# Two sums of attention weights per pair of heads: formed in the weights' own tiles, partly by DMA, with the mask of two pairs on another engine

## The chip, the cores and the metric

The kernel runs on one core of a Trainium2 chip. The metric is the device time of one execution in microseconds (us). A profiled execution also leaves a trace: the start and the length of every instruction on TensorE (PE, and PEld for its weight loads), VectorE (DVE), ScalarE (ACT), GpSimd (POOL) and SyncE (SP), and of every DMA packet.

## The reference

Hashed attention is followed by a mixing layer. Only the first part is touched by the change.

```python
# q, k, v: (4, 8, 768, 64), proj: (64, 6)
q_bucket = sum((q @ proj > 0) * 2**arange(6));  k_bucket likewise
mask   = q_bucket[..., :, None] == k_bucket[..., None, :]
scores = where(mask, q @ k.T / sqrt(64), -1e9)
attn   = exp(scores - max) / (sum(exp(scores - max)) + 1e-9)
x      = (attn @ v), heads side by side: (4, 768, 512)
# then: X = real(fft2(x)); u = x + X; un = layernorm(u)
# out = u + relu(un @ w_ch1) @ w_ch2      w_ch1: (512, 2048), w_ch2: (2048, 512), both float64
```

## The kernel before

**Pairs and chunks.** Two heads make a pair: 4 batches of 4 pairs, numbered n = 0 to 15. `attention(b)` loops over the four pairs of a batch and, in each, over six chunks c of 128 keys. One such step does this:

- `weigh(n, c)`: PE forms the transposed scores, 128 keys by 2 x 384 queries for each head (L815); ACT takes the exponential into a weights tile `pk` of 128 x 1536 numbers (L819, two instructions). The mask comes in one of two ways. For the pairs in `LITE` (0 to 4) two more matmuls per half put a very large term under the scores of matching buckets (L808). For the others DVE multiplies the weights by a comparison of bucket numbers, two instructions per chunk (L825).
- `values`: PE multiplies the previous chunk's weights by v, into two accumulating banks (L836).
- DVE adds the chunk's weights to a running sum `acc` (L898): for batch 0 in two halves of 128 x 768, later in one instruction of 128 x 1536. Five chunks are added per pair, the first being the start.
- `prepare(n + 1)`: transposes, copies and bucket bits of the next pair's q and k, spread over the steps. A pair in `LITE` needs four matmuls and six DVE instructions for its bits (L735 to L742); another needs one bank of bits, two bucket images (L764, copied at L768) and one small table `kb`.
- One slice of the float64 weights is turned into float32 by `narrow`: DVE at L603, L607 and L612, ACT at L611, L615 and L616. w1 has 16 slices, done during `attention(0)` in four of five steps; w2 has 16, done later, during `attention(1)`.

After the last chunk `scale` adds up a pair: a copy `vs` on DVE (L845), two ACT copies that wait for it (L848), four matmuls of `acc` with ones (L853), and a quotient on DVE, two times six instructions from L859 to L869.

**Tiles.** There are two weights tiles (`NPK = 2`), used in turn, and two `acc` tiles in the work pool (tag `t6`, shared with the temporaries `ef` of `fold`).

**Order.** For `attention(0)` the order on PE, DVE, ACT and POOL is the order in which the program is written. Later the order is set by a planner with priorities, where `mix(b - 1)`, the mixing layer of the batch before, runs between the steps of `attention(b)`. Each engine works through its own list in order. `fold(b, 0)` begins the mixing inside the last pair of a batch.

**Queues.** SP issues the loads of q, k and v, the constants, the first seven slices of w1 and the stores of `ad` and `bd`. POOL issues the other 9 slices of w1 and all 16 of w2 (`fetch`, L657, 512 KB each), and the output.

Of the kernel before, what the change touches and what calls it, by code (L numbers as in the profile page):

```python
# [479 lines left out]
def _main(  # L480
# [27 lines left out]
    def wt(shape, dtype, tag, name, bufs=2):  # L508
        return work.tile(shape, dtype, tag=tag, name=name, bufs=bufs)
# [44 lines left out]
    make_identity(nc, ident)  # L554


    LITE = (0, 1, 2, 3, 4)
    pjw = const.tile([P, P], F32, tag="pjw", name="pjw")
    nc.gpsimd.memset(pjw, 0.0)
    for h in range(2):  # L560
# [13 lines left out]
    norms = const.tile([P, 2, NPAIR * B], F32, tag="norms", name="norms")  # L574


    NPK = 2
    pks = []
    for i in range(NPK):
        pk = const.tile([P, 2, 2, HALF + 1], F32, tag=f"pk{i}", name=f"pk{i}")  # L580
# [52 lines left out]
    def weights(wsb, wdr):  # L633

        wide = wdr.dtype == I64
        slices = [
            (wsb[:, c, f : f + WC], wdr[c * P : (c + 1) * P, f : f + WC])
            for f in range(0, wdr.shape[1], WC)
            for c in range(wdr.shape[0] // P)
        ]  # L640
        raws, masks = [], []
        if wide:
            zt = wt([P, 3, 2 * WC], F32, "z", f"zraw{wdr.shape[0]}", 1)
            raws += [zt[:, i] for i in range(3)]
            if wsb is w1:
                ft = wt([P, 12, WC], F32, "F", "fraw", 1)
                raws += [
                    ft[:, i : i + 2].rearrange("p i w -> p (i w)") for i in range(0, 8, 2)
                ]
                masks = [ft[:, i] for i in range(8, 12)]  # L650

        def fetch(i, queue):
            if i < len(slices):
                dst, src = slices[i]
                if wide:
                    raw = raws[i % len(raws)].bitcast(I32)
                    queue.dma_start(raw.bitcast(I64), src)  # L657
                else:
                    queue.dma_start(dst, src)

        depth = len(raws) or 4
        for i in range(depth):
            fetch(i, nc.sync if wsb is w1 else nc.gpsimd)
            if wsb is w1 and i == 1:
                load(1)
        yield
        for i, (dst, src) in enumerate(slices):
            if wide:
                mask = masks[i % 4] if masks else wt([P, WC], F32, "u", f"mask{i}", 2)
                narrow(  # L670
                    dst, raws[i % len(raws)].bitcast(I32), mask.bitcast(I32),
                    i if wsb is w1 else len(slices) + i,
                )
            fetch(i + depth, nc.gpsimd)
            yield
            if wsb is w1 and i % NDC == NDC - 1:


                f = i // NDC * WC
                if f < DFF // 2:  # L680
                    centre(f, average(f))
# [13 lines left out]
    def prepare(n):  # L695

        lite = n in LITE
        act = lite and n > 0  # L700
        ts = {}
        for io, nm in enumerate("qk"):
            tn = nat.pop((nm, n))
# [55 lines left out]
        for h in range(2):  # L759
            ps = ps_sc.tile([P, 2, 512], F32, tag="sc", name=f"qb{n}_{h}")  # L760
            for g in range(2):
                rows = slice(32 * g, 32 * g + 32)
                with behind() if g + h else nullcontext():
                    last[0] = nc.tensor.matmul(  # L764
                        ps[:, g, 0:HALF], pw[rows, h, :], bt[rows, :],
                        start=True, stop=True,
                    )
            evac(qb[:, h, :].rearrange("p (g s) -> p g s", g=2), ps[:, :, 0:HALF])  # L768
        ps = ps_sc.tile([P, 2, 512], F32, tag="sc", name=f"kb{n}")
        for c in range(NT):  # L770
            g, i = divmod(c, NT // 2)
# [9 lines left out]
        )  # L781
        preps[n] = ts["q"], ts["k"], qb, kb

    npk = [0]

    AHEAD = 500

    last = [None]
# [4 lines left out]
        with tc.issue_after(last[0].ins), tc.high_priority(offset=AHEAD):  # L793
            yield

    def weigh(n, c):

        qt, kt, qb, kb = preps[n]
        ks = slice(c * P, (c + 1) * P)
        heads = [slice(h * D, (h + 1) * D) for h in range(2)]  # L800
        pk = pks[npk[0] % NPK]
        npk[0] += 1
        for g in range(2):
            qs = slice(g * HALF, (g + 1) * HALF)
            ps = ps_sc.tile([P, 2, 512], F32, tag="sc", name=f"sc{n}_{g}_{c}")
            if kb is None:
                for h, rows in enumerate(heads):
                    nc.tensor.matmul(  # L808
                        ps[:, h, 0:HALF], qb[rows, 1, ks], qb[rows, 0, qs],
                        start=True, stop=False,  # L810
                    )

            for h, rows in enumerate(heads):
                with behind() if g + h and n >= NPAIR else nullcontext():
                    last[0] = nc.tensor.matmul(  # L815
                        ps[:, h, 0:HALF], kt[rows, ks], qt[rows, qs],
                        start=kb is not None, stop=True,
                    )
            nc.scalar.activation(  # L819
                pk[:, g, :, 0:HALF], ps[:, :, 0:HALF], AF.Exp, scale=SCALE  # L820
            )
        if kb is not None:
            for h in range(2):
                w = pk[:, :, h, 0:HALF]
                nc.vector.scalar_tensor_tensor(  # L825
                    w, qb[:, h].rearrange("p (g s) -> p g s", g=2), kb[:, h, c : c + 1], w,
                    op0=ALU.is_equal, op1=ALU.mult,
                )
        return pk

    def values(n, c, pk, oos):

# [5 lines left out]
                    pk[:, g, h, 0:w], start=(c == 0), stop=(c == NT - 1),  # L838
                )

    def scale(n, oos, acc):

        x = xs[n // NPAIR][:, n % NPAIR]
        vs = wt([P, 1], F32, "vs", f"vs{n}")
        nc.vector.tensor_copy(vs, oos[0][:, HALF : HALF + 1])  # L845
        halves = [x[:, g * HALF : (g + 1) * HALF] for g in range(2)]
        for g, xg in enumerate(halves):
            nc.scalar.activation(xg, oos[g][:, 0:HALF], AF.Identity, bias=vs)  # L848
        for g, xg in enumerate(halves):

            ps = pt([P, HALF], f"sum{n}_{g}")
            for h in range(2):
                nc.tensor.matmul(  # L853
                    ps[h * D : (h + 1) * D, :], ones, acc[:, g, h],
                    start=True, stop=True,
                )

            rt = wt([P, HALF], F32, "rt", f"rt{n}_{g}", 1)
            nc.vector.transpose(rt, ps)  # L859
            rc = wt([P, HALF // 32], F32, "rc", f"rc{n}_{g}")  # L860
            nc.vector.tensor_scalar(rc, rt[:, 0:HALF:32], S * EPS, None, op0=ALU.add)
            nc.vector.reciprocal(rc, rc)
            rb = wt([P, HALF], F32, "rb", f"rb{n}_{g}", 1)
            nc.vector.tensor_copy(
                rt.rearrange("p (j i) -> p j i", i=32),
                rc[:, :, None].broadcast_to([P, HALF // 32, 32]),
            )
            nc.vector.transpose(rb, rt)
            nc.vector.tensor_tensor(xg, xg, rb, op=ALU.mult)  # L869

    def attention(b):
# [1 line left out]
        pending = []  # L873

        def finish():
            n, c, pk, oos, acc = pending.pop(0)
            with behind() if n >= NPAIR and t is not None else nullcontext():
                values(n, c, pk, oos)
            if c == NT - 1:
                scale(n, oos, acc)  # L880

        for t in range(NPAIR):
            n = NPAIR * b + t
# [2 lines left out]
                load(n + 1)  # L886
            ahead = prepare(n + 1) if n + 1 < NPAIR * B else iter(())
            oos = [ps_o.tile([P, 512], F32, tag="o", name=f"oo{n}_{g}") for g in range(2)]
            acc = wt([P, 2, 2, HALF], F32, "t6", f"acc{n}", 2)
            first = None  # L890
            for c in range(NT):
                new = weigh(n, c)
                if c == 0:
                    first = new[:, :, :, 0:HALF]
                else:

                    for g in (0, 1) if b == 0 else (slice(0, 2),):
                        nc.vector.tensor_tensor(  # L898
                            acc[:, g], (first if c == 1 else acc)[:, g],
                            new[:, g, :, 0:HALF], op=ALU.add,  # L900
                        )
                while pending:
                    finish()
                pending.append((n, c, new, oos, acc))
                if c > 2:
                    next(half, None)
                if c > 0:
                    next(ahead, None)
                yield
        t = None  # L910
        while pending:
            finish()


    HW = HALF // 2
# [22 lines left out]
    def fold(b, cp):  # L938
# [4 lines left out]
        if cp == 0:  # L943
            zs[b] = wt([P, 2, 2, 2, HALF], F32, "z", f"z{b}", 1)
        for pc in range(2):
            ef = wt([P, 2, S], F32, "t6", f"ef{b}_{cp}_{pc}", 2)
            e = ef[:, 0]
            nc.vector.tensor_tensor(
                e, x[:, cp], x[:, cp + 2], op=ALU.subtract if pc else ALU.add
# [437 lines left out]
    next(other)  # L1387
    nc.sync.dma_start(ch, cn["ch"].ap())
    nc.sync.dma_start(sq, cn["sq"].ap())


    ET = mybir.EngineType
    with tc.manual_schedule(engines={ET.PE, ET.DVE, ET.Activation, ET.Pool}):
        for _ in prepare(0):
            pass
        roomy[0] = False
        for i, _ in enumerate(attention(0)):
            if i % 5 < 4:
                next(other, None)
        for _ in other:  # L1400
            pass
        pwf = wt([P, 2, P], F32, "t6", "pwf", 2)
        nc.sync.dma_start(pwf, cn["pw"].ap())
        nc.scalar.copy(pw, pwf)
        means = []
        for f in range(DFF // 2, DFF, WC):
            means.append((f, wt([P, WC], F32, "u", f"mean{f}", 2)))
# [92 lines left out]
```

## Time and profile before

| | us |
|---|---|
| median of three runs (1154.63 to 1157.35) | 1154.7 |
| profiled execution, its own time | 1154.21 |
| its span in the trace | 1152.4 |
| PE busy | 1100.6 (96%) |
| DVE busy | 779.9 (68%) |
| ACT busy | 451.8 (39%) |
| POOL busy | 74.5 (6%) |

The span is the time from the first to the last instruction of the program; 1.8 us of the profiled execution lie around it. An engine's busy time is the union of its instructions. A busy PE is one with matmuls in its pipeline and is not PE at its peak. A mean share says little here, since the kernel has stages with different limits; the pairs of batch 0 fill the stretch from 13.6 to 138.9 us, those of batch 1 the stretch to 412.9 us, if the first exponential of a pair is taken as its start.

### The profile page before, as it was taken

To read this page: it belongs to the slowest core of one execution; us is meant where nothing else is said; L and a number is where in the kernel's file an instruction comes from. 1 tells how busy PE (TensorE), PEld (TensorE's weight loads), DVE (VectorE), ACT (ScalarE), POOL (GpSimd) and SP (SyncE) were. 2 spreads that over 40 slices of the span, in tenths; PEclk is the share of its full clock that TensorE was granted. 3 is DMA by queue.
4 is the path that set the end of the run, shared out by engine and by line. 5 is a ranking of instruction groups with operands and counts; after the bars stand their busy time and mean duration, and the time that the engine had idled before them with its cause. 6 is when DMAs were issued, how large, how long until landed. Compare 5 with 4: busy or idle time off the path is not lost. (4 is left out here: it accounts for less than half of the span.)

```text
span 1152.4 us, 13749 instructions
## 1 busy us (share of the span) xinstructions
PE 1100.6 (96%) x4921; PEld 641.9 (56%) x4921; DVE 779.9 (68%) x1373; ACT 451.8 (39%) x858; POOL 74.5 (6%) x149
## 2 busy tenths in 40 slices
PE   7989889889999999999999999999999999999996
PEld 4444355444445445644674467654575468768675
DVE  4889959837938455883857877785775877644352
ACT  6778348623222212345224531345424431340420
POOL 1000001100100010020000002002000002010002
PEclk9999999999999999999999999999999999999998
DMA  9534135514611014113042315013104204131401
GB/s 272 151 80 121 40 93 168 167 44 146 224 48 47 17 32 152 28 51 106 15 151 68 86 52 177 15 42 96 47 31 139 64 28 164 48 96 56 154 24 39
DMA packets 131661, 103.11 MB, mean 89 GB/s; under 512 B 81280, under 2 KB 120320, under 8 KB 131584
## 3 DMA queue, kind: packets, MB, share of 16 engines
q1 hardware_dynamic: 123984, 82.35, 24.5%
q0 software_dynamic: 6032, 19.40, 5.1%
q8 instruction: 41, 0.67, 0.2%
q10 hardware_dynamic: 1568, 0.39, 0.2%
q14 instruction: 36, 0.29, 0.1%
HBM read 81.14 MB, written 20.97 MB: 89 GB/s over the span
## 5 line engine op out<-in xcount | busy, mean ns | idle before, releaser
L1214 PE MATMUL o<-w,h 128*128 128x256 f32 x864 | 194.0, 381 | 0.0
L819 ACT ACTIVATE pk<-sc 128x768 f32<-128x768 f32 x192 | 147.8, 808 | 101.2 <-PE sc L815 81.6
L1214 PEld LDWEIGHTS o<-w,h 128*128 128x128 f32 x864 | 162.3, 190 | 30.2 <-issue 3.4
L825 DVE SCALAR_TENSOR_TENSOR pk<-qb,kb,pk 128x768 f32<-128x768 bf16 x132 | 129.3, 1013 | 38.6 <-ACT pk L819 38.5
L815 PE MATMUL sc<-qt,kt 64*128 64x384 f32 x768 | 152.9, 501 | 0.9 <-ACT pk L819 0.9
L836 PE MATMUL oo<-pk,vn 128*64 128x385 f32 (+1 forms) x768 | 149.3, 498 | 1.8 <-DVE pk L825 1.8
L1314 PE MATMUL h_p<-x,w 128*128 128x384 f32 x384 | 140.2, 494 | 2.1 <-ACT qt L531 0.6
L898 DVE TENSOR_TENSOR acc<-acc,pk 128x1536 f32<-128x1536 f32 (+1 forms) x80 | 113.3, 1433 | 9.8 <-ACT pk L819 8.9
L1314 PE MATMUL h_p<-w 128*128 128x384 f32 x288 | 106.3, 492 | 2.9 <-ACT qt L531 1.8
L1314 PEld LDWEIGHTS h_p<-x,w 128*128 128x128 f32 x384 | 69.7, 190 | 56.5 <-ACT h L1346 3.4
L836 PEld LDWEIGHTS oo<-pk,vn 128*64 128x64 f32 x768 | 47.8, 136 | 90.5 <-issue 73.0
L1083 PE MATMUL h<-x,w 128*128 128x384 f32 x256 | 88.6, 499 | 4.1 <-DVE h L1089 3.1
L815 PEld LDWEIGHTS sc<-qt,kt 64*128 64x128 f32 x768 | 66.8, 186 | 44.7 <-issue 23.2
L1065 PE MATMUL o<-w,h 128*128 128x512 f32 x192 | 85.2, 596 | 0.6 <-DVE rt L859 0.6
L1314 PEld LDWEIGHTS h_p<-w 128*128 128x128 f32 x288 | 53.1, 190 | 43.4 <-ACT qt L531 2.4
L1083 PEld LDWEIGHTS h<-x,w 128*128 128x128 f32 x256 | 48.1, 193 | 40.6 <-issue 5.0
L1065 PEld LDWEIGHTS o<-w,h 128*128 128x128 f32 x192 | 35.5, 190 | 43.8 <-issue 41.7
L926 POOL DMA_DIRECT2D out_dram<-w x30 | 16.5, 552 | 468.7 <-issue 426.6
L1226 DVE SCALAR_TENSOR_TENSOR w<-o,rs,w 128x256 f32<-128x256 f32 x42 | 20.1, 481 | 32.2 <-PE o L1214 32.2
L1244 ACT COPY w<-o 128x256 f32<-128x256 f32 x18 | 6.7, 372 | 81.7 <-PE o L1214 81.7
L988 PE MATMUL cs<-ch,z 128*128 128x128 f32 (+3 forms) x192 | 31.8, 316 | 4.7 <-ACT kt L531 2.6
L1214 PE MATMUL o<-w 128*128 128x256 f32 x144 | 34.6, 383 | 1.2 <-DVE u L1226 0.9
(159 smaller groups left out, 1320.3 us busy)
## 6 DMA issues: line engine op xcount, KB each, us to landing
w<-ad SPq DMA_DIRECT2D x168, 128.0 KB, 2.0
w<-bd SPq DMA_DIRECT2D x42, 512.0 KB, 4.4
zraw<-in_moe_w_ch_dram POOLq DMA_DIRECT2D x21, 512.0 KB, 4.1
vn<-in_v_dram SPq DMA_DIRECT2D x32, 192.0 KB, 3.3
qn<-in_q_dram SPq DMA_DIRECT2D x31, 192.0 KB, 3.3
kn<-in_k_dram SPq DMA_DIRECT2D x31, 192.0 KB, 3.3
ad<-st SPq DMA_DIRECT2D x8, 512.0 KB, 3.7
bd<-st SPq DMA_DIRECT2D x8, 512.0 KB, 3.5
```

The costliest lines, as they stand in the source:

```text
L815: last[0] = nc.tensor.matmul(ps[:, h, 0:HALF], kt[rows, ks], qt[rows, qs], start=kb is not None, stop=True,)
L819: nc.scalar.activation(pk[:, g, :, 0:HALF], ps[:, :, 0:HALF], AF.Exp, scale=SCALE)
L825: nc.vector.scalar_tensor_tensor(w, qb[:, h].rearrange("p (g s) -> p g s", g=2), kb[:, h, c : c + 1], w, op0=ALU.is_equal, op1=ALU.mult,)
L836: nc.tensor.matmul(oos[g][h * D : (h + 1) * D, 0:w], nat["v", n][:, c, h, :], pk[:, g, h, 0:w], start=(c == 0), stop=(c == NT - 1),)
L898: nc.vector.tensor_tensor(acc[:, g], (first if c == 1 else acc)[:, g], new[:, g, :, 0:HALF], op=ALU.add,)
L926: nc.gpsimd.dma_start(out[b, s0 : s0 + 2 * w - 1 : 2, cols], src[at : at + w, cols])
L988: nc.tensor.matmul(ps[:, pc + 2 * lo : pc + 2 * hi - 1 : 2], z[:, cp, pc, par, t * P : (t + 1) * P], ch[:, cp, pc, lo:hi], start=(cp == 0) ...
L1065: nc.tensor.matmul(ps, hr, w2[:, fc, cols], start=(i == 0), stop=(i == len(rows) - 1))
L1083: nc.tensor.matmul(ps, w1[:, c, fc * P : (fc + 1) * P], x[:, c, g * HALF : (g + 1) * HALF], start=(c == 0), stop=(c == NDC - 1),)
L1214: nc.tensor.matmul(ps, a[:, r], right7[i][:, r], start=start and r == 0, stop=r == HF // 2 - 1, skip_group_check=not start,)
L1226: nc.vector.scalar_tensor_tensor(t[:, cols], src, r, t[:, cols], op0=ALU.mult, op1=ALU.add)
L1314: nc.tensor.matmul(ps, ring[n % NR][:, k], right[i][:, k], start=start and k == 0, stop=k == 1, skip_group_check=not start,)
```

## The change

Four weights tiles take the place of two. Each pair gets them in the order `four(n)`: the first two hold chunks 0 and 1 and become the sums `acc` and `acc2`; the other two hold chunks 2 and 3 and then 4 and 5; the next pair has the two halves exchanged. For pairs 0 to 5 (`QUEUED`) chunks 2, 3 and 4 are added to their sum by an accumulating DMA that POOL issues (in pair 3 only chunks 2 and 3), the remaining chunks by DVE, and at the end of the pair DVE adds `acc2` to `acc`. From pair 6 on DVE adds all five chunks, into the first tile. The sums' matmuls and the quotient come one step later than before: `scale` stops at a `yield`, and `advance` lets it go on after the next chunk's scores.

`LITE` loses pairs 2 and 3: they are masked by DVE, their bits are prepared in the other way, and the table `pw` that this needs is loaded and cast early. The copy `vs` goes from DVE to ACT. The copies of bucket images of pairs 1 to 4 go to ACT. Every `fetch` is issued by SP. `ef` gets a tag of its own with one buffer.

```diff
-    LITE = (0, 1, 2, 3, 4)
+    LITE = (0, 1, 4)
+    QUEUED = range(6)
...
-    NPK = 2
+    NPK = 4
...
-        def fetch(i, queue):
+        def fetch(i):
...
-                    queue.dma_start(raw.bitcast(I64), src)
+                    nc.sync.dma_start(raw.bitcast(I64), src)
...
-            fetch(i + depth, nc.gpsimd)
+            fetch(i + depth)
...
-        act = lite and n > 0
+        act = 0 < n <= NPAIR
...
-            evac(qb[:, h, :].rearrange("p (g s) -> p g s", g=2), ps[:, :, 0:HALF])
+            evac(qb[:, h, :].rearrange("p (g s) -> p g s", g=2), ps[:, :, 0:HALF], act)
...
-    def weigh(n, c):
+    def weigh(n, c, pk):
...
-    def scale(n, oos, acc):
+    def scale(n, oos, acc, rest):
...
-        nc.vector.tensor_copy(vs, oos[0][:, HALF : HALF + 1])
+        nc.scalar.copy(vs, oos[0][:, HALF : HALF + 1])
...
+        for g in range(2) if rest else ():
+            w = acc[:, g, :, 0:HALF]
+            nc.vector.tensor_tensor(w, w, rest[:, g, :, 0:HALF], op=ALU.add)
+        yield
...
             if c == NT - 1:
-                scale(n, oos, acc)
+                quotients.append(scale(n, oos, four(n)[0], rest))
+                next(quotients[-1])
+
+        quotients = []
+
+        def four(n):
+            return pks[2 * (n % 2) :] + pks[: 2 * (n % 2)]
+
+        def advance():
+            for sc in list(quotients):
+                if next(sc, True):
+                    quotients.remove(sc)
...
-            acc = wt([P, 2, 2, HALF], F32, "t6", f"acc{n}", 2)
-            first = None
+            acc, acc2, *others = four(n)
             for c in range(NT):
-                new = weigh(n, c)
-                if c == 0:
-                    first = new[:, :, :, 0:HALF]
-                else:
-
-                    for g in (0, 1) if b == 0 else (slice(0, 2),):
-                        nc.vector.tensor_tensor(
-                            acc[:, g], (first if c == 1 else acc)[:, g],
-                            new[:, g, :, 0:HALF], op=ALU.add,
-                        )
+                pk = (acc, acc2, *others, *others)[c]
+                to = acc if c else None
+                if n in QUEUED:
+                    to = (None, None, acc, acc2, acc, acc2)[c]
+                queued = n in QUEUED and 1 < c < (NT - 2 if t == NPAIR - 1 else NT - 1)
+                weigh(n, c, pk)
+                advance()
                 while pending:
                     finish()
-                pending.append((n, c, new, oos, acc))
+                if to is not None:
+                    new, to = pk[:, :, :, 0:HALF], to[:, :, :, 0:HALF]
+                    if queued:
+                        nc.gpsimd.dma_start(to, new, accum_op=ALU.add)
+                    for g in () if queued else (0, 1) if b == 0 else (slice(0, 2),):
+                        nc.vector.tensor_tensor(to[:, g], to[:, g], new[:, g], op=ALU.add)
+                pending.append((n, c, pk, oos, acc2 if n in QUEUED else None))
...
+        while quotients:
+            advance()
...
-            ef = wt([P, 2, S], F32, "t6", f"ef{b}_{cp}_{pc}", 2)
+            ef = wt([P, 2, S], F32, "ef", f"ef{b}_{cp}_{pc}", 1)
...
+    pwf = wt([P, 2, P], F32, "u", "pwf", 2)
+    nc.sync.dma_start(pwf, cn["pw"].ap())
...
+            if i == 4:
+                nc.scalar.copy(pw, pwf)
...
-        pwf = wt([P, 2, P], F32, "t6", "pwf", 2)
-        nc.sync.dma_start(pwf, cn["pw"].ap())
-        nc.scalar.copy(pw, pwf)
```

More of the change, by code (lines that the diff above doesn't have):

```diff
@@ L656, in fetch @@
                     raw = raws[i % len(raws)].bitcast(I32)
-                    queue.dma_start(raw.bitcast(I64), src)
+                    nc.sync.dma_start(raw.bitcast(I64), src)
                 else:
-                    queue.dma_start(dst, src)
+                    nc.sync.dma_start(dst, src)
         depth = len(raws) or 4
         for i in range(depth):
-            fetch(i, nc.sync if wsb is w1 else nc.gpsimd)
+            fetch(i)
             if wsb is w1 and i == 1:
@@ L782, in prepare @@
         preps[n] = ts["q"], ts["k"], qb, kb
-    npk = [0]
     AHEAD = 500
@@ L800, in weigh @@
         heads = [slice(h * D, (h + 1) * D) for h in range(2)]
-        pk = pks[npk[0] % NPK]
-        npk[0] += 1
         for g in range(2):
@@ L828, in weigh @@
                 )
-        return pk
     def values(n, c, pk, oos):
@@ L853, in scale @@
                 nc.tensor.matmul(
-                    ps[h * D : (h + 1) * D, :], ones, acc[:, g, h],
+                    ps[h * D : (h + 1) * D, :], ones, acc[:, g, h, 0:HALF],
                     start=True, stop=True,
@@ L875, in finish @@
         def finish():
-            n, c, pk, oos, acc = pending.pop(0)
+            n, c, pk, oos, rest = pending.pop(0)
             with behind() if n >= NPAIR and t is not None else nullcontext():
```

## The prediction, made before the changed kernel ran

> **What bounds the kernel now.** The page comes first. Over the whole span PE looks like the limit, but section 2 shows two stretches in which it is not alone.
>
> ```profile
> PE 1100.6 (96%) x4921; PEld 641.9 (56%) x4921; DVE 779.9 (68%) x1373; ACT 451.8 (39%) x858; POOL 74.5 (6%) x149
> ...
> PE   7989889889999999999999999999999999999996
> ...
> DVE  4889959837938455883857877785775877644352
> ...
> DMA  9534135514611014113042315013104204131401
> ```
>
> But for the last slice, PE's digits below 9 end before the tenth (28.8 us each). All that the change touches in quantity, pairs 0 to 5, lies there, so I cut that stretch at the pairs' first exponentials (13.6, 40.4, 72.4 and 99.0 us), at the sum matmuls of pair 3 (128.8) and at turns of the load after that, and asked for the busy time by stretch. Columns: stretch, its length, then busy us of PE, PEld, DVE, ACT, POOL, with the clock, DMA share and GB/s last.
>
> ```profile
> 13.60:40.40 26.80, 25.92 (x144) 11.83 (x142) 18.93 (x29) 22.81 (x42) 2.32 (x4) 1.00 0.88 282
> 40.40:72.40 32.00, 29.36 (x162) 13.13 (x160) 27.33 (x50) 24.03 (x44) 2.61 (x5) 1.00 0.38 103
> 72.40:99.00 26.60, 25.35 (x150) 11.29 (x148) 25.19 (x45) 23.98 (x47) 0.04 (x1) 1.00 0.35 91
> 99.00:128.80 29.80, 25.20 (x146) 11.09 (x144) 26.45 (x53) 17.35 (x33) 0.11 (x1) 1.00 0.36 93
> ...
> 144.00:156.00 12.00, 7.89 (x54) 3.94 (x50) 6.82 (x10) 5.94 (x12) 0.00 (x0) 1.00 0.59 154
> ...
> 174.00:228.00 54.00, 49.03 (x204) 25.91 (x201) 50.60 (x88) 40.17 (x76) 6.89 (x13) 1.00 0.51 156
> 228.00:240.00 12.00, 8.87 (x29) 4.50 (x28) 5.06 (x10) 3.32 (x7) 0.00 (x0) 0.86 0.45 167
> 240.00:1152.00 912.00, 887.79 (x3845) 536.98 (x3844) 591.29 (x1037) 297.21 (x571) 59.57 (x107) 1.00 0.26 77
> ```
>
> Pair 0 is PE's and has a slack DVE (7.9 us). Pairs 2 and 3, up to the sums, are DVE's: 51.6 of 56.4 us busy. After 240 us it is PE's alone. Hence the rule for everything below: the end moves by what PE loses or wins in idle time before 240 us; work taken from PE where DVE sets the pace wins nothing.
>
> The prices come from the groups of pairs 0 to 3 (13 to 140 us) and of the page:
>
> ```profile
> L898 DVE TENSOR_TENSOR acc<-acc,pk 128x768 f32<-128x768 f32 x32 | 29.2, 953 | 4.7 <-ACT pk L819 4.7
> L848 ACT ACTIVATE x<-oo,vs 128x384 f32<-128x384 f32 x8 | 4.2, 577 | 10.8 <-DVE vs L845 10.8
> ```
> ```profile
> L825 DVE SCALAR_TENSOR_TENSOR pk<-qb,kb,pk 128x768 f32<-128x768 bf16 x132 | 129.3, 1013 | 38.6 <-ACT pk L819 38.5
> ...
> w<-ad SPq DMA_DIRECT2D x168, 128.0 KB, 2.0
> w<-bd SPq DMA_DIRECT2D x42, 512.0 KB, 4.4
> zraw<-in_moe_w_ch_dram POOLq DMA_DIRECT2D x21, 512.0 KB, 4.1
> ```
>
> An add of one chunk is 1.8 us in batch 0 (two of 953 ns, overlapping a little), a mask 2.0 us (two of 1013), and ACT waits 10.8 us in four pairs for a copy of one column, because that copy stands behind DVE's backlog.
>
> **What the Trainium skill says.** TensorE: Matmul & The Clock Gate (Specifications) calls the queues of ScalarE, VectorE and GpSimd strict first-in first-out; the trace agrees (the 10.8 us). DMA: Bandwidth & Descriptors (SWDGE vs HWDGE vs iDMA) ties accumulation to DMAs issued by GpSimd, and (SDMA does more than copy) describes it as an addition of two streams; no trace here shows one. The same page (Anatomy of one DMA) fits 2.0 us plus bytes over 436e3: for one chunk (128 x 1536 x 4 = 786,432 bytes) an estimate of 3.8 us.
>
> **The accumulating DMA, bounded.** From 2.0 us for 128 KB and 4.1 for 512 KB a copy of 768 KB would land in 5.5 us (5.5 ns per KB). If the second stream that is read, the destination, costs as much again per byte, 9.7 us. Range 3.8 to 9.7, I take 7: between copy and double. A gain below nothing is excluded, as somebody waits.
>
> **The change, part by part.**
>
> *DVE in pairs 2 and 3, the main term.* Masks: + 2 x 6 x 2.03 = + 24.4 us. Adds in this stretch: 10 before; after, chunk 5 of pair 2, chunks 4 and 5 of pair 3, and the joining of the two sums of pairs 1, 2 and 3, six in all: - 7.3. Bits of pair 3: four of 0.61, two of 0.26 and two of the k side become one of 0.55 and a small copy of 0.2: - 2.0. Sum + 15.1, so 66.7 us of work where 56.4 were spent. Even with no idle DVE that is 10.3 us more.
>
> *The new wait.* Chunk 4 is written into chunk 2's tile, so its exponential waits for mask 2 and then for the DMA. Queued behind it on ACT are everything of the later steps: the narrowing that DVE waits for, and the next scores on PE, whose banks ACT must empty. Working pair 2 from its first exponential along the written order: mask 0 ends at 3.5, the joining of pair 1 at 5.3, a narrowing (1.8) at 7.1, mask 1 at 9.1, the quotient of pair 1 (5.3, twice six instructions) at 14.4, a narrowing at 16.2, mask 2 at 18.2, mask 3 at 20.2. The DMA issued at 18.3 lands at 25.3; ACT was free at 18.3, DVE runs dry at 22.6. Then mask 4, the narrowing, mask 5, add 5, and the pair is 35.9 long, since chunk 4's DMA, issued at 28.9, frees the next pair's first tile. In pair 3, worked likewise (its fold is 3.2 us twice), the sums start 39.5 after its first exponential. Together 75.4 against 56.4: + 19. With 3.8 for the DMA it is 31.4 and 39.2: + 14.2. Price: + 14 to + 19, I take + 17.
>
> *Pair 1.* DVE loses 5 - 2 adds (5.5) and 2 us of bits: it had 27.3 of 32, and no longer sets the pace. ACT then does: 24.0 busy plus two bucket copies (1.6), and PE has 29.4 less 1.5. From chunk 2's exponential to chunk 4's ACT's own work takes 8.2 us, of which 6.5 are left for the DMA: a stall of half a us at 7, two or three times. I take 29.5, - 2.5.
>
> *Pair 0.* The adds saved were in DVE's slack: 0. But DMA is at 0.88 there, and chunk 2's sum must land in about 7 us beside the weights: 0 to + 4, I take + 1.
>
> *PE.* 24 pairs of mask matmuls, 0.16 us apart, and 3 us of bits less: 7 us, in a stretch that DVE sets: 0. A pair of scores of pair 4 goes ahead of pair 3's sums in the new order: three halves of 0.8, - 2.4.
>
> *Pairs 4 and 5.* Five adds of 1.75 become two of 1.8, per pair - 5.1 on DVE. Of 8.7 us of adds between 174 and 228, 3.6 stay. PE idles there 5.0, at 144 to 156 another 4.1 (it waits for copies of q and k queued behind adds), and at 228 to 240 3.1, where DVE waits for the slices of w2 to land. I credit half of the 12.2: - 6, bounds - 2 and - 12.
>
> *The copy vs on ACT.* 16 x 0.15 us move; the waits of 10.8 us end, but lie where ACT was not last: 0.
>
> *Queues.* 25 fetches (9 of w1, 16 of w2) leave POOL, where each took 0.53 us to issue, and stand on SP among the loads of q, k and v. q of pair 2, issued at 24.3 before, follows the slice freed at about 27, its use is near 47; k and v follow the slices freed at 31 and 39, wanted near 51 and 73. The cover is these 12 us and more; gone, ACT and PE would wait 3 us per load. POOL keeps 17 accumulations, in turn, then the memset of `F` and the stores, long after. `pw`'s load (0.4 us cast in pair 0's slack step) and `ef`'s single buffer (DVE writes and reads it itself) cost nothing. From pair 6 on five adds remain: 0.
>
> Sum: + 17 - 2.5 + 1 - 2.4 - 6 = + 7.1, rounded to + 8 because pairs 0 to 5 can also meet waits that I have not listed. Against the profiled execution's 1154.2 (span 1152.4 and 1.8 around it) 1162; its distance from the median, 0.5, I ignore.
>
> **The rivals.** *The relief decides (faster).* Place: 144 to 240 us. If pairs 2 and 3 pack without idle DVE (+ 10.3) and 10 of the 12.2 us come back: 10.3 - 2.5 - 2.4 - 10 = - 4.6, 1150. It decides once the DMAs land within 4 us, so that ACT never waits. For: DVE is at 94% from 174 to 228, and PE idle beside it. Against: the idle of 228 to 240 is a landing, which less DVE work doesn't hasten. *The DMAs are slow.* At 9.7 us each: pair 0 + 3, pair 1 two waits of 3.2, pairs 2 and 3 two of 2.7, to + 8: 1177. For: the second stream, the full DMA queues until 36 us. *The parts cancel*: the relief at 9 and the loss at + 14 give 1154. *The order isn't what it says*: excluded, the changed program's order has the 17 accumulations and 24 more mask instructions on DVE.
>
> **How the numbers follow.** Forecast (1155 to 1170) 0.55, slow DMAs 0.15, relief 0.17, cancelled 0.13. 0.3% is 3.5 us, about what a measurement of this kernel can tell from no change. Faster 0.17, same 0.13, slower 0.70. The range 1149 to 1177 reaches from the relief to the slow DMAs.
>
> **What would show it.** Right: DVE over 90% busy from pair 2's first exponential to pair 3's sums, that stretch 70 to 76 us long; waits of ACT's `pk` for a DMA; pair 1 near 30 us; PE idle up there. Wrong: that stretch under 62 us, or a landing under 4 us with no such wait, or PE idle nearly gone between 144 and 240.

## The result: 4% slower, and the profile after

The changed kernel takes 1202.37 us, the median of its runs (1200.86 to 1205.25), against 1155.55 for the kernel before in the same session: a ratio of 1.041 (95% interval 1.038 to 1.043). The direction was forecast, the size was not: + 8 was predicted, + 47 came, and the range ended at 1177.

The page of the kernel after, first its totals and slices (30.0 us each), then rows of its queues, its groups and its DMA issues (KB each, median us from issue to landing):

```profile
PE 1117.7 (93%) x4893; PEld 646.2 (54%) x4893; DVE 764.5 (64%) x1347; ACT 455.7 (38%) x878; POOL 75.9 (6%) x143
...
PE   7777787989999999999999999999999999999996
...
DVE  4547882872782836577575688777576688545343
...
PEclk9897998999999999999999999999999999999999
DMA  9886626691461101412215231502204121330511
...
q0 software_dynamic: 11408, 19.67, 8.3%
...
L823 DVE SCALAR_TENSOR_TENSOR pk<-qb,kb,pk 128x768 f32<-128x768 bf16 x156 | 152.6, 1010 | 59.4 <-ACT pk L817 59.3
...
w<-ad SPq DMA_DIRECT2D x168, 128.0 KB, 2.0
w<-bd SPq DMA_DIRECT2D x42, 512.0 KB, 4.4
pk<-pk POOLq DMA_DIRECT2D x17, 768.0 KB, 9.7
zraw<-in_moe_w_ch_dram SPq DMA_DIRECT2D x24, 512.0 KB, 5.0
```

PE's digits are 7 or 8 in the first seven slices, its clock digits vary from 7 to 9 there (210 us), and the DMA engines stay at 6 or more for 270 us with one exception, where the kernel before stood at 1 to 5 after its first slice. The 17 new DMAs land after 9.7 us in the median, the end of the prediction's bounds. DVE is *less* busy in total than before: 24 more masks (156 for 132), at 1010 ns each, cost less than the adds, bits and copies that left it. From the tenth slice on PE is at 9 but for the last slice, as before.

The stretches of the kernel after, cut at the first exponentials of pairs 0, 1, 2 and 3, at the sum matmuls of pair 3 (165.65) and at the first exponentials of pairs 5 and 6; columns as in the prediction:

```profile
12.70:49.27 36.57, 30.04 (x152) 13.49 (x150) 13.46 (x24) 23.11 (x44) 4.06 (x3) 0.91 1.05 278
49.27:83.72 34.45, 28.45 (x162) 12.13 (x160) 18.69 (x37) 25.47 (x47) 3.81 (x3) 0.95 0.79 166
83.72:125.45 41.73, 29.83 (x142) 11.21 (x142) 32.13 (x50) 25.51 (x49) 3.83 (x3) 0.84 0.62 122
125.45:165.65 40.20, 30.46 (x135) 11.61 (x135) 33.93 (x57) 20.63 (x38) 2.67 (x3) 0.92 0.48 96
165.65:220.00 54.35, 45.46 (x245) 25.34 (x244) 27.80 (x60) 21.43 (x41) 3.84 (x3) 0.94 0.55 123
220.00:305.30 85.30, 75.97 (x288) 39.60 (x286) 54.63 (x97) 41.62 (x81) 3.87 (x3) 0.96 0.54 140
305.30:1200.00 894.70, 870.76 (x3757) 528.23 (x3755) 579.20 (x1017) 293.55 (x575) 52.42 (x107) 1.00 0.27 79
```

In pairs 2 and 3 up to the sums DVE has 32.13 + 33.93 = 66.1 us of work, as the prediction said (66.7), but in 81.9 us: it is busy for 81%, not for over 90. In these two pairs DVE waits for one thing alone, an exponential of ACT:

```profile
DVE pk L823 <- ACT pk L817: 13.0, 6, 4.9
```

In no stretch before 305 us is PE, DVE or ACT busy for 90%. Set beside the same cuts of the kernel before, the 48.5 us of span lie here:

| stretch | before | after | measured | predicted |
|---|---|---|---|---|
| start to pair 0's first exponential | 13.6 | 12.7 | - 0.9 | 0 |
| pair 0 | 26.9 | 36.6 | + 9.7 | + 1 |
| pair 1 | 32.0 | 34.5 | + 2.5 | - 2.5 |
| pair 2 to the sums of pair 3 | 56.4 | 81.9 | + 25.5 | + 17 |
| from there to pair 6 | 135.0 | 139.7 | + 4.7 | - 2.4 - 6 |
| pair 6 to the end | 888.6 | 895.6 | + 7.0 | 0 |

What ACT waited for from 12 to 165 us (us in total, times, longest), the waits of the kernel after:

```profile
ACT pk L817 <- DMA pk<-pk: 30.0, 8, 5.8
ACT qt L531 <- PE trq L711: 12.0, 6, 5.7
ACT pk L817 <- PE sc L813: 7.0, 5, 3.5
```

The first line is the wait that the change brings: an exponential (L817) stands until an accumulating DMA has read the tile that it writes. 13.1 of the 30.0 us are in pair 0 and 12.9 in pairs 2 and 3, where DVE's 13.0 us stand behind them. Another wait comes in pair 4, between 180 and 200 us. There `kn`, pair 6's k, is asked for by the tile; the kernel after first, then the same load of the kernel before, between 140 and 175 us:

```profile
L543 SPq DMA_DIRECT2D kn<-in_k_dram x2: 1310/1394/1477, 185.4 to 186.7; - x2
...
  DMA kn<-in_k_dram: 10.4, 1
...
DMA to landing us min/median/max: 6.7/8.4/10.2
```
```profile
L543 SPq DMA_DIRECT2D kn<-in_k_dram x2: 592/620/647, 150.3 to 150.9; - x2
...
DMA to landing us min/median/max: 3.3/3.3/3.3
```

Two accumulations were issued at 181.8 and 186.9 us, around this load. Its second half lands in 10.2 us instead of 3.3, ACT stands 10.4 us at the square of k (L692), and the copies to `F` and the matmuls that read them stand behind it (PE idle 7.5 us at `cs`). The prediction had no line for a load that a transfer makes late.

### The profile page after: what moved, and what is told of

The parts are those of the page before. It is cut to its first block, busy times and chain, and to the rows that moved or that the text cites. A ratio compares the mean times of both kernels' runs of the same rounds, so it can differ in the third digit from the quotient of the medians.

```text
span 1200.9 us, 13678 instructions
## 1 busy us (share of the span) xinstructions
PE 1117.7 (93%) x4893; PEld 646.2 (54%) x4893; DVE 764.5 (64%) x1347; ACT 455.7 (38%) x878; POOL 75.9 (6%) x143
## 3 DMA queue, kind: packets, MB, share of 16 engines
q0 software_dynamic: 11408, 19.67, 8.3%
## 5 line engine op out<-in xcount | busy, mean ns | idle before, releaser
L817 ACT ACTIVATE pk<-sc 128x768 f32<-128x768 f32 x192 | 147.7, 808 | 136.7 <-PE sc L813 80.2
L823 DVE SCALAR_TENSOR_TENSOR pk<-qb,kb,pk 128x768 f32<-128x768 bf16 x156 | 152.6, 1010 | 59.4 <-ACT pk L817 59.3
L833 PE MATMUL oo<-pk,vn 128*64 128x385 f32 (+1 forms) x768 | 163.6, 513 | 4.3 <-DVE pk L823 3.7
L813 PE MATMUL sc<-qt,kt 64*128 64x384 f32 x768 | 157.5, 520 | 3.6 <-ACT pk L817 2.5
L833 PEld LDWEIGHTS oo<-pk,vn 128*64 128x64 f32 x768 | 52.1, 140 | 103.7 <-issue 65.1
L921 DVE TENSOR_TENSOR pk<-pk,pk 128x1536 f32<-128x1536 f32 (+1 forms) x62 | 100.0, 1620 | 12.3 <-ACT pk L817 11.2
L1334 PEld LDWEIGHTS h_p<-x,w 128*128 128x128 f32 x384 | 70.6, 190 | 56.0 <-ACT h L1356 3.0
L1085 PEld LDWEIGHTS o<-w,h 128*128 128x128 f32 x192 | 35.5, 190 | 43.8 <-issue 42.4
L946 POOL DMA_DIRECT2D out_dram<-w x30 | 16.5, 552 | 493.8 <-issue 451.1
L1008 PE MATMUL cs<-ch,z 128*128 128x128 f32 (+3 forms) x192 | 32.4, 322 | 10.9 <-DVE F L1021 9.4
L1008 PEld LDWEIGHTS cs<-ch,z 128*128 128x128 f32 x192 | 28.1, 197 | 18.5 <-DVE F L1021 11.4
```

The lines of the kernel that those rows point to most:

```text
L813: last[0] = nc.tensor.matmul(ps[:, h, 0:HALF], kt[rows, ks], qt[rows, qs], start=kb is not None, stop=True,)
L817: nc.scalar.activation(pk[:, g, :, 0:HALF], ps[:, :, 0:HALF], AF.Exp, scale=SCALE)
L823: nc.vector.scalar_tensor_tensor(w, qb[:, h].rearrange("p (g s) -> p g s", g=2), kb[:, h, c : c + 1], w, op0=ALU.is_equal, op1=ALU.mult,)
L833: nc.tensor.matmul(oos[g][h * D : (h + 1) * D, 0:w], nat["v", n][:, c, h, :], pk[:, g, h, 0:w], start=(c == 0), stop=(c == NT - 1),)
L921: nc.vector.tensor_tensor(to[:, g], to[:, g], new[:, g], op=ALU.add)
L946: nc.gpsimd.dma_start(out[b, s0 : s0 + 2 * w - 1 : 2, cols], src[at : at + w, cols])
```

## The experiments

Three explanations compete. **Masks** (M in some expectations): DVE's 24 more instructions set the pace of pairs 2 and 3. **Waiting** (W): ACT, and PE's sums, wait for the accumulating DMAs. **Contention** (C): the DMAs take the DMA engines' time from loads that others wait for. In the table are the medians in us; the kernel before took 1155.5, 1155.4 and 1155.2 in the three sessions. "Both undone" keeps the rest of the change: the four tiles, the later sums, `vs` on ACT and the fetches on SP.

| kernel | time | ratio, 95% interval |
|---|---|---|
| changed kernel | 1202.37 | 1.0382 to 1.0431 |
| adds on DVE | 1170.96 | 1.0106 to 1.0153 |
| masks of pairs 2, 3 on PE | 1189.57 | 1.0265 to 1.0322 |
| both undone | 1152.23 | 0.9961 to 0.9986 |
| six tiles | 1191.99 | 1.0289 to 1.0338 |
| copies for accumulations | 1169.38 | 1.0113 to 1.0145 |
| both undone + 11 DMAs nobody waits for | 1160.35 | 1.0023 to 1.0067 |
| both undone + DMAs of pairs 0 to 3 | 1184.27 | 1.0246 to 1.0277 |
| both undone + DMAs of pairs 4, 5 | 1160.20 | 1.0028 to 1.0058 |
| both undone, sums at once | 1143.94 | 0.9892 to 0.9919 |
| changed kernel, sums at once | 1197.95 | 1.0349 to 1.0381 |
| before + fetches on SP | 1147.06 | 0.9926 to 0.9959 |
| before + `vs` on ACT | 1153.08 | 0.9973 to 0.9991 |

**1 to 3. Which of the two parts.** Adds back on DVE, masks back on PE, and both:

```diff
-    QUEUED = range(6)
+    QUEUED = ()
```
```diff
-    LITE = (0, 1, 4)
+    LITE = (0, 1, 2, 3, 4)
```

> The changed kernel with no pair queued: DVE does all adds, into the first tile; four tiles, masks of pairs 2 and 3 on DVE, fetches on SP stay. Theory W (the accumulating DMAs hold up the kernel: ACT waits 33.4 us for them in the changed kernel's trace, loads land late beside them, 10.4 us of waiting for one k load, and PE runs at half clock after each stop): all of this goes, DVE gets 9 us of adds more in pairs 2 and 3 than the changed kernel, so about 1175 us (1168 to 1182), with no stop of ACT over 5 us before 200 us but those for DVE. Theory M (the masks make DVE the limit, the DMA waits only stand where DVE would have been waited for anyway): adding adds to a full DVE makes it slower than the changed kernel, 1205 to 1215 us.

> The changed kernel with pairs 2 and 3 masked on PE again, DMA adds kept. Theory M: the 24 us of masks go, and most of the loss with them, 1160 to 1170 us. Theory W: the DMAs still land after 7 to 14 us, the waits for them stay in pairs 0, 1, 4 and 5 and are as long in 2 and 3, so only the masks' own part of the chain goes: 1185 to 1195 us.

> The changed kernel with neither DMA adds nor the masks on DVE: left are four tiles, sums in place, the one-column copy on ACT, quotients a step later, and all fetches on SP. Both theories: near before, 1150 to 1158 us. If the fetches on SP cost by themselves (third theory, Q: loads of q, k and v queue behind slices), 1160 to 1175 us.

Against both undone, masks alone cost 1170.96 - 1152.23 = 18.7 us, the DMAs alone 37.3 (with the joining adds, and with the adds that DVE is spared), and together 50.1, 6 less than the sum. The DMAs are the larger cause, twice the masks; in the prediction DVE's work made most of the sum, and the DMAs a few us of it. The masks' price is near what was worked out, 66.7 + 7.3 - 56.4 = 17.6 us of work more on DVE if DVE also adds. The stretches of the kernel with DVE adds, pair 2 and then pair 3 up to its sums:

```profile
69.90:105.60 35.70, 28.04 (x132) 10.58 (x134) 34.37 (x52) 25.56 (x49) 0.00 (x0) 0.86 0.29 77
105.60:147.65 42.05, 31.99 (x140) 12.48 (x136) 38.70 (x64) 20.11 (x37) 0.11 (x1) 0.88 0.21 54
```

DVE works 73.1 of 77.8 us (94%) there, and waits for ACT only 0.6 us: here it does set the pace. The DMA adds took 7 us of that work away and the stretch grew by 4.1, to 81.9.

**4. Take the wait for the tile away.** Six weights tiles for pairs 0 to 3, so that no chunk of a pair is written over one that a DMA of the same pair still reads:

```diff
+    more = []
+    for i in range(2):
+        pk = w2.rearrange("p c f -> p (c f)")[:, i * 4 * DM : i * 4 * DM + 4 * (HALF + 1)]
...
+        more.append(pk)
...
         def four(n):
+            if n < NPAIR:
+                return [(pks + more)[(2 * n + 4 + i) % 6] for i in range(6)]
```

> The changed kernel with six weights tiles for pairs 0 to 3 (two of them in the still empty space of the second weight matrix), so that chunks 4 and 5 and the next pair's first do not wait for a landing; the DMAs, their number and bytes are the same. If the wait for the tile is what costs (W1): the waits of pairs 0 to 3, 29 us of ACT, go, and some 20 to 30 us with them: 1172 to 1185 us. If it is the DMA engines' time, taken from other loads (W2): at most 8 us better, 1194 to 1203 us. Theory M: DVE's 15 us more of work stay, 1185 to 1200 us.

10.4 us came back of 50. The time lies in the range that was named for the masks and 2 us below that for the engines' time, so it decides little by itself. The wait did go: over the whole span ACT's waits of `pk` for a DMA fell from 33.4 us to 3.9, and pair 0 is back at 26.8 us. But pairs 1 and 4 are longer than in the changed kernel (38.0 and 59.9), and other waits took over. PE's waits from 12 to 165 us in this kernel (its lines are six higher, L861 are the sums, L855 is the joining add; the second row is the same wait for a tile in w2's space):

```profile
PE sum L861 <- DVE pk L855: 9.6, 2, 6.4
PE sum L861 <- DVE w L855: 6.0, 1, 6.0
```

The sums wait for the joining add, and that stands on DVE behind the adds of the last chunks, one of which waits 9.9 us for a transfer into the same sum to land. Further tiles move the wait from the tile's reuse to the pair's end. ACT also waits 25.3 us for transposes of q on PE. So this run does not separate waiting from contention.

**5. The same bytes without the addition.**

```diff
-                        nc.gpsimd.dma_start(to, new, accum_op=ALU.add)
+                        nc.gpsimd.dma_start(to, new)
...
-            nc.vector.tensor_scalar(rc, rt[:, 0:HALF:32], S * EPS, None, op0=ALU.add)
+            nc.vector.tensor_scalar(rc, rt[:, 0:HALF:32], 1.0, None, op0=ALU.add)
```

> The changed kernel, but each of the 17 accumulating DMAs is a plain copy of the same 768 KB between the same tiles, at the same place in the order; the weights of the earlier chunk are overwritten instead of added up, so the denominators lack them (and get + 1.0 instead of the small constant). All waits and all other work stay. Question: what of the + 47 us is due to the addition inside the DMA, what to moving 768 KB at all? If the addition costs a second read (landing near 5.5 us alone instead of 7.1, and less of the queues' time), the waits of ACT for a transfer fall from 33 us to 10 to 18 and the time to about 1180 to 1190. If the addition is free and the bytes are what costs, landing stays within 1 us of 7.1 alone and 9.7 median, and the time stays within 5 us of 1202.

This kernel leaves out the addition, so its sums lack the weights of the chunks that are copied over. The time falls by 33.0 us, below the range that was expected: 1169.38, 1.6 under the kernel with DVE adds. So even transfers at the price of a copy would have gained next to nothing over adding on DVE. Two rows of its page:

```profile
q0 software_dynamic: 5696, 19.67, 4.9%
...
pk<-pk POOLq DMA_DIRECT2D x17, 768.0 KB, 5.9
```

and the answers on `pk` and POOL, of the kernel after and then of the copies (ns of one issue, min/median/max; how long ACT waited; then the landings):

```profile
L919 POOL DMA_DIRECT2D pk<-pk x17: 1270/1279/1503, 22.9 to 261.4; - x17
...
  ACT pk L817: 33.4, 9
...
DMA to landing us min/median/max: 7.1/9.7/14.2
```
```profile
L919 POOL DMA_DIRECT2D pk<-pk x17: 748/751/938, 23.6 to 230.4; - x17
...
  ACT pk L817: 8.7, 5
...
DMA to landing us min/median/max: 4.0/5.9/9.6
```

With little beside it, an accumulation lands in 7.1 us and a copy in 4.0. Queue q0 also holds the output stores, which take 1.7% of a 1142 us span where no such DMA is issued: 19.4 us. What is left, 8.3% of 1200.9 less 19.4 = 80.3, is 4.7 us of all 16 DMA engines per accumulation; for a copy, from 4.9% of 1165.7, it is 2.2. So the addition doubles the engines' time. Its packets are smaller too, but that isn't the reason: in the traces' packet records one of 1536 bytes that accumulates takes 139 ns, one of 4608 bytes that is copied 198, and a plain one of 1024 bytes on SP's queue 46. Per byte, accumulating takes twice as long as either. By stretch, the accumulation costs over the copy + 6.3 in pair 0, + 5.1 in pair 1, + 8.0 from pair 2 to pair 3's sums, and + 16.5 from there to pair 6.

**6 and 9. Waiting or contention.** The same 11 transfers of pairs 0 to 3, at the same places, once with nobody waiting and once adding up the weights. Both kernels are "both undone" otherwise. In the first, `decoys` are five tiles in the still empty space of w2, and POOL copies one column to time each transfer:

```diff
+                if n < NPAIR and 1 < c < (NT - 2 if t == NPAIR - 1 else NT - 1):
+                    s, d = decoys[c - 2], decoys[3 + c % 2]
+                    nc.gpsimd.tensor_copy(s[:, 0, 0, 0:1], pk[:, 1, 1, HALF - 1 : HALF])
+                    nc.gpsimd.dma_start(
+                        d[:, :, :, 0:HALF], s[:, :, :, 0:HALF], accum_op=ALU.add
+                    )
```
```diff
-    LITE = (0, 1, 4)
+    LITE = (0, 1, 2, 3, 4)
...
-    QUEUED = range(6)
+    QUEUED = range(4)
```

> The kernel with both parts undone (1152.2), with 11 accumulating DMAs of 768 KB added in pairs 0 to 3, released at the moments at which chunks 2 to 4 are weighed, between tiles that nobody else reads or writes; nobody waits for one. POOL copies one column to time each, and five memsets on POOL come at the start. Theory C (the transfers take the DMA engines' time from the loads of weights, q, k and v): the time rises by 10 us or more, pair 0 grows from 26.9 to over 30 us, and loads of q and k land later than in the kernel without decoys (3.4 us mean). Theory W (the cost is in waiting for the tile that a transfer reads): within 3 us of 1152.2, and pairs 0 to 3 keep their lengths of 26.9, 31.8, 25.8 and 37.5.

> The kernel with both parts undone (1152.2), with the accumulating DMAs of pairs 0 to 3 put back (11 of the 17; pairs 4 and 5 add on VectorE). The same transfers at the same places cost + 8.1 when nobody waits for them. Theory W + C (the wait for the tile, and for the joined sum, costs more than the time taken from the loads): + 22 to + 32, so 1174 to 1184, with waits of ACT's exponentials for a transfer of 20 us or more. Theory C alone: + 6 to + 12, so 1158 to 1164. With + 8 for the six of pairs 4 and 5 the parts should add up to about the + 37 of all 17.

8.1 us with nobody waiting, 32.0 when the sums are used: the difference, some 24 us, is what waiting for them costs, less what DVE gains by the adds it is spared. Both bounds of the expectation for the unused transfers were missed: contention is there, but below 10 us, and pair 0 keeps its 26.9 us although their landings in it are 12.9, 12.5 and 10.9 us. So pair 0's + 9.7 in the changed kernel is waiting, for transfers that land late beside the weights. ACT's two largest waits of pairs 0 to 3 in the kernel that uses the sums:

```profile
ACT pk L817 <- DMA pk<-pk: 32.4, 9, 6.3
ACT pk L817 <- PE sc L813: 4.8, 5, 2.7
```

and, in the one where nobody waits for a transfer, ACT's waits for loads in pair 3 (98 to 143 us), which grows by 7.1 us:

```profile
ACT sq L697 <- DMA qn<-in_q_dram: 6.0, 1, 6.0
ACT sq L697 <- DMA kn<-in_k_dram: 4.0, 1, 4.0
```

This is contention by itself: from 36 to 215 us k's loads take 9.2 us there in the mean, against 3.4 in the same kernel without the transfers.

**8. Pairs 4 and 5 alone.** `QUEUED = (4, 5)` with the masks on PE.

> The kernel with both parts undone, but with the accumulating DMAs kept in pairs 4 and 5 alone (six of 17). Theory C: the wait of ACT for k of pair 6 (10.4 us in the changed kernel) comes back, pair 4 grows from 41.9 to between 50 and 60 us, the time to 1160 to 1168. If pair 4's loss in the changed kernel was handed on from pairs 0 to 3 (later slices of w2, PE clock at half), pair 4 stays below 45 us and the time within 4 us of 1152.2; if the relief of VectorE there wins, as the prediction had it, the time falls below 1149.

The six DMAs cost 8.0 us where a gain of 6 was forecast: no relief shows. But pair 4 is 42.4 us long: the expected 50 to 60 did not come. k of pair 6 is asked for 11 us into the pair here, beside one accumulation, lands in 7.9 us, and ACT waits 3.9 for it; in the changed kernel 24 us into the pair, beside two, and ACT waits 10.4. Contention's price depends on what the loads happen to fall beside. The profiled execution was the fastest of this kernel (1156.8), and its stretches show only part of the 8 us, so the rest is not located. On top of those of pairs 0 to 3, the six cost 5.3 us (1189.57, where all 17 are queued and PE masks, less 1184.27).

**7 and 10. The later sums.** The sums at once after a pair's last values, without and with the two parts:

```diff
                 next(quotients[-1])
+                advance()
```

> The kernel with both parts undone, and the sums and the quotient of a pair follow its last values at once, as in the kernel before, instead of after the next pair's first chunk. In the changed order pairs 9, 11 and 13 are each 1.4 us longer than before, in every variant. If the later place of the sums causes that, those pairs come back by 1.4 us each and the time falls by 4 to 6 us, to about 1147. If it has another cause (the order of loads on SP), the time stays within 2 us of 1152.2. If the later place is what brings pairs 0 to 3 their gain, it rises by 2 to 6 us.

> The changed kernel, with the sums and the quotient of each pair at once after its last values, as in the kernel before, instead of one chunk of the next pair later. If the later place costs what it cost without masks and DMAs (8.3 us), the time falls to 1192 to 1196, pairs 9, 11 and 13 by 1.4 us each. If the later place is what the joining add of the queued pairs needs (PE's sums would stand at it, ahead of the next pair's chunk), pairs 0 to 5 lose 1 to 2 us each, and the time stays within 4 us of 1202.

Without the two parts it is 8.3 us faster, more than expected, and at 1143.94 the fastest kernel of the study, 1% under the kernel before. With them it is 4.4 faster, half of that; pair 6 to the end is then 888.2 us, the kernel before's 888.6. Thus the + 7.0 in the last row of the table of stretches is the later sums, in full (what they hold up there was not looked for); in pairs 1 to 3 putting them back costs a little (37.3 for 34.5 in pair 1), so the whole is less.

**11 and 12. Two edits priced at nothing.** In the kernel before, all fetches on SP, and `vs` on ACT:

```diff
-        def fetch(i, queue):
+        def fetch(i, queue=nc.sync):
...
-            fetch(i + depth, nc.gpsimd)
+            fetch(i + depth)
```
```diff
-        nc.vector.tensor_copy(vs, oos[0][:, HALF : HALF + 1])
+        nc.scalar.copy(vs, oos[0][:, HALF : HALF + 1])
```

> The kernel before, with one edit: the 25 fetches of w1 and w2 that GpSimd issued stand on SP. The prediction priced this at nothing. If that holds, within 1.5 us of 1155.5. If the fetches delay the loads of q, k and v behind them, slower by 3 us or more; if they start or land earlier (GpSimd took 0.5 us for each issue and shares its turn), faster by 2 to 6 us. The four tiles, the copy of the value column on ScalarE and these fetches together gave - 11.6.

> The kernel before, with one edit: the 16 copies of one column (`vs`) are made on ScalarE and not on VectorE. The prediction priced this at nothing, though it ends waits of ScalarE for VectorE of 10.8 us in pairs 0 to 3. If those waits lie where ScalarE isn't last, the time stays within 1.5 us of 1155.5. If they hold up the next pair's scores, it falls by 3 to 10 us.

The fetches gain 8.1 us, - 3.9 of it between pair 3's sums and pair 6 and - 2.1 after; what makes it faster was not traced. `vs` gains 2.1. Both gains lie hidden under the loss; the prediction had put both at zero.

## Why the prediction was right and wrong

The step that failed is the price of the transfers. Each was priced nearly as if it were alone, at 7 us and mostly hidden, and without its effect on the loads of others; they landed after 9.7 us in the median, and k's loads after 9.0 where 3.7 had been usual.

*DVE's work, right.* 66.7 us were worked out for pairs 2 and 3, 66.1 measured; with DVE adds (66.7 + 7.3 = 74.0) 73.1.

*The landing, where it failed first.* The bounds 3.8 to 9.7 held for one transfer alone, and 7 is what one alone takes (7.1); that was partly luck, for the copy from which the 7 was reckoned was put at 5.5 and takes 4.0. The Trainium skill's fit (DMA: Bandwidth & Descriptors, Anatomy of one DMA), an estimate of 3.8, fits the plain copy (4.0) and not the accumulation. The page's section SDMA does more than copy lists an operation that reduces two streams; the doubled time per byte agrees with a second stream, though no run shows its reads. The error was to price each DMA alone. The written order issues the next one 3 to 5 us after the first (142.0 and 145.5 us in pair 3), within its flight: the first lands in 7.8, the second in 10.4. Beside pair 0's weights it is 13.6 and 14.2. So the upper bound was the median.

*The main term, right in form and short by the landing.* The prediction's own working for pair 2 to pair 3's sums gives 70.6 at 3.8 us and 75.4 at 7; its rival adds 5.4 at 9.7: 80.8. Measured: 73.9 with copies that land in 4.4 to 5.6 there, and 81.9 with landings of 7.8 to 10.9. So most of what + 25.5 exceeds + 17 by goes with that one number. The excess lies in pair 2 (41.7 for the 35.9 that were worked out; pair 3 to its sums took 40.2 for 39.5), where PE's clock was also lowest (0.84); the two were not separated. The expected waits of ACT's `pk` came; DVE above 90% did not, since DVE stood 13.0 us behind them (with copies 5.0, with DVE adds 0.6). At 75.4 us the working itself gave only 66.7 / 75.4 = 88%.

*Pair 0, + 9.7 for + 1, and pair 1, + 2.5 for - 2.5.* The prediction saw the full DMA queues in pair 0 and allowed at most 4 us for them. ACT's three waits there come to 13.1. Pair 1 has 7.3 us of waits where one and a half were allowed.

*The relief of pairs 4 and 5, the step with the wrong sign.* "I credit half of the 12.2: - 6" assumed that transfers already hidden stay hidden. The cover named for SP's loads, 12 us between issue and use, was checked against the fetches moved to SP and never against the accumulations on the DMA engines, which is where it broke (k's loads, 9.0 us for 3.7 in the mean between 36 and 215 us). With copies the stretch from pair 3's sums to pair 6 is 123.2 us long, 11.8 under before; with accumulations 139.7. Only 3.8 of the 11.8 show against the kernel with DVE adds, where the stretch is 126.9 long.

*Costs put at nothing.* The later sums: credited with - 2.4 by pair 4's scores, and + 7.0 from pair 6 on, where the statement was "From pair 6 on five adds remain: 0". Fetches and `vs`: 0, in truth - 8.1 and - 2.1 in the kernel before.

*The clock, not priced.* PE runs at half clock for 44.4 us of the first 320, in the kernel before for 3.4, in stretches of 3.4, 6.8 or 10.2 us. The Trainium skill (TensorE: Matmul & The Clock Gate, Part 1: The HAM clock gate) says that after an idle window of about 3.4 us PE gets half its rate. The length agrees, but the window need not be idle throughout: by the trace PE was busy for 0.0 to 1.6 of the 3.4 us ahead of each of the nine stretches, and not at all ahead of three of them. So waits that starve PE can bring it on, whatever caused them: the kernel with DVE adds has 27.3 us of it, both undone 13.7. At half clock for 41.0 us more than before, PE can have lost at most 20.5 us, an estimate from these figures; how many of the 47 are due to it was not isolated.

*The rivals.* "The DMAs are slow" named the right mechanism; its 1177 lacks 7 us in pair 0, 13 between pair 3's sums and pair 6 and the 7 of the later sums, which together make 1204 (measured 1202.4). The relief and the cancelling fell.

## What to carry to other kernels

Price an accumulating DMA by what it does beside its neighbours: ask when the next one is issued, what else the engines carry then, and which loads with a tight use stand beside it; a transfer that takes work off a busy engine can still set the pace through a tile, a sum or someone else's load. A new DMA load on the engines spends the cover of all other transfers, so "hidden before" has to be worked out again for each of them. And test the small edits of a large change one by one: here two that were put at nothing gained 10 us, which the large ones hid.

## What the runs showed of the hardware

- 768 KB from SBUF to SBUF: copied in 4.0 us with little beside it, accumulated in 7.1; of all 16 DMA engines 2.2 and 4.7 us; POOL's issue 0.75 and 1.28 us; (5696 - 2432) / 17 = 192 and (11408 - 2432) / 17 = 528 packets, 2432 being those of the stores. An accumulating packet of 1536 bytes took 139 ns, a plain one of 1024 bytes 46.
- Accumulations in flight slow the loads of another queue two- to threefold: k's 192 KB, issued on SP's queue, landed in 9.2 us in the mean instead of 3.4 where nobody waited for the accumulations. In the changed kernel SP's issue of such a load beside two accumulations took 1.3 to 1.5 us instead of 0.6.
- PE's clock was halved after 3.4 us in which PE was busy for at most 1.6 us, not only after 3.4 us without a matmul.
- Moving 25 issues of 512 KB from POOL's queue to SP's made the kernel before 0.4 to 0.7% faster.
